# Windowed attention and a softplus feed-forward: every engine's order after slot 22 comes from a list scheduler in the kernel

## The chip, the cores and the metric

One core of one Trainium2 chip runs the whole program. The metric is the device time of one execution in microseconds (us). The kernel before took 929.23 us, the median of 3 runs (927.66 to 931.1).

## The reference, cut to what matters

```python
B, H, S, D = 8, 8, 576, 64           # float32; 4608 tokens in all
scores = q @ k.T / sqrt(D)           # per batch and head
# heads 0-3: the last 32 keys; heads 4-7: every 4th of the last 128 keys
attn = softmax(where(mask[h], scores, -1e9))
x = (attn @ v), heads side by side   # 4608 x 512
h = x @ w_in                         # 512 x 2048
g = maximum(h, 0) + log1p(exp(-abs(h)))
out = g @ w_out                      # 2048 x 512
```

## The kernel before, in words

The 4608 tokens are nine chunks of 512. A chunk has four attention groups (two heads each), 36 groups in all. A float32 matmul operand is split into a high and a low fp32r part, so a product is three matmuls: high by high, high by low, low by high. TensorE (PE) is the engine with the most work. W_in and W_out come in as 16 blocks (ff = 0 to 15) of 128 columns or rows.

**Chunks 0 to 2** run in 48 slots, (chunk, ff) pairs in the order of `RUNS`. A slot i is 12 matmuls of 512 columns for h (`h_part`, four times three) and 12 for the output of slot i - 2 (`o_part`, `LAG` = 2). Between them ScalarE (ACT) takes abs, exp and log of h, VectorE (DVE) makes softplus from them, ACT copies the high part gh, DVE subtracts to the low part gl. Chunks 0 and 1 leave their accumulators half way (`kept_part`, DRAM tile `kept`) and resume later (`resumed_part`). Slots 0 to 9 and all decoding of weights in that time follow the hand-written string `OPENING`.

**Chunks 3 to 8** run in three double passes (d = 0 to 2), two chunks at once. Each pass has eight pairs p; a pair has seven products (`product`, six matmuls each; seven instead of eight quarter products, by sums and differences of blocks of x and of W_in), whose results DVE takes out of two PSUM banks h_x and h_y into `temps`, `hs` or `stored` (`aside`). The output matmuls (`late_o`, 12 per use u of a W_out block) run beside them in the first half and alone in the second. The sums and differences of x (`combine`, `split_high`, `split_low`) must stand before the first pair of a pass; those of W_in (`weight_sum`, `weight_13`, `weight_24` on GpSimd, POOL, then copies on ACT and DVE) are made once per pair: pairs 0 to 3 during the slots (`EARLY` = 4), the rest during the first pass, then kept in DRAM and loaded for passes 1 and 2. W_out blocks are kept in DRAM by `keep_w_out` and streamed back into free buffers (`feed`, `used`).

**Attention** of groups 8 to 35 is done in visits. Visit n puts the scores of group n and the weighted values of group n - 1 into two halves of the same two PSUM banks `sv_ps`: 64 small matmuls of scores, then 64 of values. After it DVE scales and masks (`maximum`, L431) and takes maxima (L440), ACT takes eight exponentials (L448), DVE divides (L460, L463, L466) and transposes 32x32 blocks (L488); SP sends them to DRAM (`send`) and, when they have landed, brings them back rearranged (`bring`, four DMAs to tile pt). Visit n + 1 needs that pt for its values.

**What sets the order.** Every instruction of these engines stays in the order in which the kernel emits it, on its engine. The kernel before emits by clocks written by hand. `at(when, part)` puts a part on a heap by slot number, `pump` emits what is due, `tick` and `do_chores` add chores (decoding, sums, splits) while an estimated backlog of DVE is under 0.4 us. `attend` places the parts of a visit at fixed offsets; visits come every 3.3 slots (groups 8 to 11), 2.7 slots (groups 13 to 20), then every 20 us by `in_beats`. The output of a finished chunk leaves by `finished` (L1128): two column halves share one tile `ob` at a time ("w5_1", "x_d" for chunk 2), so the second pair of copies waits until the DMAs of the first have read it. All DMAs but two go through SP's queue, which waits for the semaphores of one DMA before it goes on to the next.

```python
at(clock(7.0 if quick else 5.5), g.divisor, cost=0.36)      # L959
at(clock(8.8 if quick else 8.2), send, n)                   # L965
at(clock(12.4 if quick else 13.0), bring, n)                # L966
```

Of the kernel before, what the change touches and what calls it, by code (L numbers as in the profile page):

```python
# [50 lines left out]
EARLY = 4  # L51
# [45 lines left out]
def tile_windowed_attention_softplus_ffn(  # L97
# [189 lines left out]
    def raw_block(d, name, kt):  # L287

        c = FIRST + 1 + 2 * d
        if name == "s1":  # L290
            if (d, kt) not in ones:
                if d == 0:
                    ones[d, kt] = const.tile([P, CH], F32, name="sums", tag=("g_x", "g_y")[kt])
                else:
                    if kt == 0:
                        ones[d] = const.tile([P, 2, CH], F32, name="sums", tag="w14_0")
# [31 lines left out]

    def blocks_of(d):

        def split(name):
            parts = []
            for kt in range(2):
                for cost, part in ((0.0, split_high), (0.69, split_low)):
                    chore = lambda part=part, kt=kt: part(d, name, kt)
                    chore.block = d, name
                    parts.append((cost, chore))
            return parts

        sums = lambda name: [(0.69, lambda kt=kt: combine(d, name, kt)) for kt in range(2)]  # L340
        before = split("a11") + split("a12")
        behind = sums("s1") + sums("s3") + sums("s2") + split("s2") + sums("s4")
        for name in ("s3", "s1", "a22", "s4"):
            behind += split(name)
        return before, behind
# [8 lines left out]
    class Group:  # L354
# [60 lines left out]
        def maximum(self):  # L415
# [24 lines left out]
            pin(nc.vector.tensor_reduce(out=nm, in_=self.blocks, axis=AX.X, op=ALU.max, negate=True))  # L440

        def exponentials(self):
            self.sm = wk.tile([P, NB], F32, name="sm")
            for t in range(NB):
# [76 lines left out]
        def weighted(self, shared=None):  # L521
# [24 lines left out]
            if self.c >= FIRST:  # L546
                self.x = x_half(self.c, self.pr // 2)[:, self.pr % 2], None, src
                return
# [14 lines left out]
        def x_high(self):  # L563
            for dh, _, src in self.x_parts():
# [107 lines left out]
    def ob_tiles(c, resumed=False):  # L672

        tags = ("x_c", "x_d")
        if resumed:
            tags = ("xh10", "xh11") if c else ("g_x", "g_y", "x_d")
        for m in range(NKT):
            if len(tags) == 3 and m < 2:
                obs[m] = const.tile([P, CH], F32, name="ob", tag=tags[m])
                continue  # L680
            if m % 2 == 0:
                obs["both"] = const.tile([P, 2, CH], F32, name="ob", tag=tags[-1] if m else tags[0])
            obs[m] = obs["both"][:, m % 2]
        for m in range(NKT if resumed else 0):
            load_dma(out=obs[m], in_=kept[c, m])

    def o_part(i, m):
# [5 lines left out]
        resumed = final and c < FIRST and ff == NFF - 1  # L693
        if first:
            o_ps[m] = bank(f"o_ps{m}", f"o{m}")
        if m == 0:
            if final and not resumed and c < FIRST:
                ob_tiles(c)
# [6 lines left out]
        if final and resumed:  # L705
            at(now[0] + 0.12, resumed_part, m, c, o_ps[m], cost=0.69)
        elif final and c == FIRST:
            at(now[0] + 0.25, finished, m, c, o_ps[m], cost=0.0 if m % 2 else 0.69)
        elif final and i + LAG <= OPENED:
            keeping[m] = c, o_ps[m]  # L710
        elif final:
            at(now[0] + 0.12, kept_part, m, c, o_ps[m])

    STEP = 2 / 7
# [66 lines left out]
    BEATS = 2 * NPAIR  # L781
# [6 lines left out]
    def weight_sum(p, j):  # L788
# [591 lines left out]
```

## Time and profile before

| what | value |
|---|---|
| median of 3 runs | 929.23 us (927.66 to 931.1) |
| the profiled execution | 932.48 us |
| its span, first to last instruction | 930.7 us |
| PE busy | 872.7 us, 94% of the span |
| DVE, ACT busy | 557.8 us (60%), 551.6 us (59%) |
| POOL busy | 56.0 us (6%) |
| moved by DMA | 177.54 MB, 191 GB/s over the span |
| mean granted TensorE clock | 0.967 |

The span is what the profiler sees between the first and the last instruction; the execution's own time is 1.8 us longer. A matmul's end is modelled, and matmuls overlap, so the busy time of PE holds more than its work: a matmul of 512 columns is shown with 0.39 us but starts 0.227 us after the one before it. The granted clock is 1 where TensorE ran at 2.4 GHz and 0.5 where it ran at 1.2 GHz; a mean between them says for what part of the stretch it was low.

### The profile page before, as it was taken

The numbers are of one execution on the slowest core, as the hardware profiler recorded it, in microseconds if no ns is written. First come the engines' busy times: TensorE is split into PE (matmuls) and PEld (weight loads), VectorE is DVE, ScalarE is ACT, GpSimd is POOL, SyncE is SP. The second block draws the span as 40 slices with busy tenths as digits, with TensorE's granted clock in tenths as the row PEclk, the third lists the DMA queues.
The fourth block names the chain that finished last, engine by engine and source line by source line (L and its number), as shares of the span: only waits on it lengthen the run. The fifth ranks groups of instructions, "written<-read, shape, count | busy, mean of one in ns | idle before, by whom it ended". The sixth has DMA issues, their size and how long they took to land.

```text
span 930.7 us, 19972 instructions
## 1 busy us (share of the span) xinstructions
PE 872.7 (94%) x7997; PEld 704.9 (76%) x7997; DVE 557.8 (60%) x950; ACT 551.6 (59%) x1354; POOL 56.0 (6%) x58
## 2 busy tenths in 40 slices
PE   6999999998998999899997799999998999999798
PEld 3788778886776887677875688778876888888686
DVE  5788978744544657766664555656655635555422
ACT  6888768764565666667565345666664435655421
POOL 0000000300004201431000000000000000000000
PEclk7899989999998999999999899999998999999999
DMA  7788725676657523766566646767743526562052
GB/s 245 252 258 266 244 68 190 193 259 226 205 173 257 202 82 117 264 225 225 171 205 231 211 147 190 265 227 250 259 151 128 182 80 205 190 204 69 23 203 91
DMA packets 91773, 177.54 MB, mean 191 GB/s; under 512 B 10144, under 2 KB 26656, under 8 KB 91680
## 3 DMA queue, kind: packets, MB, share of 16 engines
q1 hardware_dynamic: 91392, 175.86, 56.8%
q8 instruction: 63, 1.03, 0.4%
q10 hardware_dynamic: 288, 0.41, 0.1%
q14 instruction: 30, 0.25, 0.1%
HBM read 134.28 MB, written 41.94 MB: 189 GB/s over the span
## 4 chain that ended last, share of the span: by engine, by line
PE 71%; ACT 11%; DMA 8%; DVE 7%; issue 2%; SPq 1%; POOL 0%; DVEq 0%; ACTq 0%; POOLq 0%
PE o_ps L203 35%; PE h_ps L203 13%; PE h_x L203 9%; PE h_y L203 8%; PE sv_ps L203 5%; ACT s L448 3%; ACT e L1118 2%; DMA out_t<-ob 2%; DMA pt<-turned 2%; DMA raw<-w 2%; ACT e L1117 2%; ACT e L1119 2%; ACT gh L657 1%; DVE gl L663 1%; DVE hs L1113 1%
## 5 line engine op out<-in xcount | busy, mean ns | idle before, releaser
L203 PE MATMUL o_ps<-gh,t 128*128 128x512 f32 (+1 forms) x776 | 270.6, 396 | 19.5 <-DVE ob L1135 9.9
L203 PEld LDWEIGHTS o_ps<-gh,t 128*128 128x128 f32 x776 | 148.6, 192 | 53.3 <-ACT gh L657 11.7
L203 PE MATMUL o_ps<-gl,t 128*128 128x512 f32 (+1 forms) x388 | 153.5, 396 | 0.7 <-DVE gl L663 0.7
L203 PE MATMUL o_ps<-gh,parts 128*128 128x512 f32 x384 | 132.9, 402 | 0.0
L203 PE MATMUL h_ps<-xh,parts 128*128 128x512 f32 x384 | 132.6, 403 | 0.0
L203 PEld LDWEIGHTS o_ps<-gl,t 128*128 128x128 f32 x388 | 74.5, 192 | 17.7 <-DVE gl L663 2.5
L203 PEld LDWEIGHTS h_ps<-xh,parts 128*128 128x128 f32 x384 | 74.1, 193 | 16.0
L203 PEld LDWEIGHTS o_ps<-gh,parts 128*128 128x128 f32 x384 | 74.2, 193 | 16.0
L203 PE MATMUL o_ps<-gl,parts 128*128 128x512 f32 x192 | 76.5, 398 | 0.0
L203 PE MATMUL h_ps<-xl,parts 128*128 128x512 f32 x192 | 76.3, 397 | 0.0
L448 ACT ACTIVATE s<-s,nm 128x64 f32<-128x64 f32 x224 | 74.7, 336 | 1.4 <-DVE nm L440 0.4
L657 ACT CAST gh<-stored 128x512 fp32r<-128x512 f32 x48 | 29.8, 621 | 70.6 <-PE o_ps L203 70.5
L663 DVE TENSOR_TENSOR gl<-hs,gh 128x512 fp32r<-128x512 f32 x48 | 33.8, 704 | 62.1 <-ACT gh L657 61.6
L663 DVE TENSOR_TENSOR gl<-stored,gh 128x512 fp32r<-128x512 f32 x48 | 33.1, 690 | 59.9 <-ACT gh L657 59.8
L203 PE MATMUL h_x<-s,t 128*128 128x512 f32 x216 | 58.3, 407 | 11.2 <-DVE hs L1113 8.0
L1117 ACT ACTIVATE e<-hs 128x512 f32<-128x512 f32 x48 | 30.3, 631 | 64.9 <-DVE stored L1123 50.2
L1118 ACT ACTIVATE e<-e 128x512 f32<-128x512 f32 x96 | 60.7, 632 | 3.1
L1119 ACT ACTIVATE e<-e 128x512 f32<-128x512 f32 x96 | 60.7, 632 | 3.1
L203 PE MATMUL h_y<-s,t 128*128 128x512 f32 x216 | 56.1, 395 | 1.5 <-DVE temps L1113 0.7
L203 PEld LDWEIGHTS h_x<-s,t 128*128 128x128 f32 x216 | 40.5, 192 | 22.4 <-DVE hs L1113 10.1
L657 ACT CAST gh<-hs 128x512 fp32r<-128x512 f32 x48 | 29.3, 611 | 37.9 <-DVE hs L1123 37.9
L1117 ACT ACTIVATE e<-stored 128x512 f32<-128x512 f32 x48 | 30.2, 629 | 33.5 <-DVE stored L1113 32.5
(110 smaller groups left out, 1441.3 us busy)
## 6 DMA issues: line engine op xcount, KB each, us to landing
t<-w_out SPq DMA_DIRECT2D x132, 256.0 KB, 3.2
raw<-w SPq DMA_DIRECT2D x64, 256.0 KB, 4.6
v<-vp SPq DMA_DIRECT2D x28, 512.0 KB, 5.5
q<-qp SPq DMA_DIRECT2D x36, 256.0 KB, 3.8
turned_over<-w_one SPq DMA_DIRECT2D x18, 512.0 KB, 4.4
t<-w SPq DMA_DIRECT2D x18, 512.0 KB, 3.7
turned_over<-w_two SPq DMA_DIRECT2D x18, 512.0 KB, 4.4
w_out<-parts SPq DMA_DIRECT2D x16, 512.0 KB, 5.3
```

The lines of the kernel that those rows point to most:

```text
L203: return tc.keep_in_program_order(nc.tensor.matmul(**kw))
L448: pin(nc.scalar.activation(out=self.blocks[:, t], in_=src, func=AF.Exp, bias=self.nm[:, t : t + 1], scale=1.0 / 8.0 if self.masked else 1. ...
L657: pin((copy or nc.scalar.copy)(out=gh, in_=ready[i]))
L663: pin(nc.vector.tensor_tensor(out=gl, in0=e, in1=gh.bitcast(F32), op=ALU.subtract))
L1113: pin(nc.vector.tensor_tensor(out=dst, in0=banks[b], in1=temps[temp], op=ALU.add))
L1117: pin(nc.scalar.activation(out=e, in_=h, func=AF.Abs))
L1118: pin(nc.scalar.activation(out=e, in_=e, func=AF.Exp, scale=-1.0))
L1119: pin(nc.scalar.activation(out=e, in_=e, func=AF.Ln, bias=1.0))
```

## The change

The hand clocks now end at slot 22 (`HANDED`). Up to there the order is emitted as before, but visits 8 to 11 come every 2.95 slots instead of 3.3, and the writes of `keep_w_out` that began at slot 18 are gone from there. From slot 22 on, all remaining work is declared as tasks: engine, cost in us, the tasks it depends on, a rank, a ring of buffers that it takes. A loop then plays time forward. At each moment every free engine takes the open task of the lowest rank, and emits it, so each engine's order is that of the played times. PE chooses among three lists: the next visit if it is open and at least `VISIT_EVERY` = 14 us after the last; else the list of outputs (`second`) if it has fallen behind the count `upto` of the next h or product, else h and products (`first`); if the chosen list's head isn't open, the other. The played times use 0.227 us for a matmul, 0.62 to 0.71 us for an ACT or DVE instruction of 512 columns, and for a DMA 0.32 MB per us one after the other and 2.3 us to land. Writes that nobody waits for soon (rank 2 and over) start only while no DMA is under way in the played time.

Homes change too. The copies of a finished chunk go to two tiles ("w5_1" and "w3_1"), one for each pair of copies. `bring_kept` fetches the kept halves of chunk 0 to "g_x", "g_y" and the ring "a". The x tiles of chunks 3 to 8 take tags c, d, a, b instead of a, b, c, d. The sums of W_in for pairs from `EARLY` on use "x_a" and "x_b" instead of "x_c" and "x_d", and `EARLY` falls from 4 to 2. The number and shapes of the matmuls stay.

```diff
@@ -48,7 +48,9 @@
 HALF = CH // 2
 NPAIR = NFF // 2
 SQ = 32
-EARLY = 4
+EARLY = 2
+HANDED = 22
+VISIT_EVERY = 14.0
 NEG = -1.0e9
 DEPTH = 4
 THIN = 90
@@ -264,7 +266,7 @@
 
     def x_half(c, k):
         if (c, k) not in x_full:
-            tag = "x_" + "abcd"[2 * ((c - FIRST - 1) % 2) * (c > FIRST) + k]
+            tag = "x_" + ("abcd" if c == FIRST else "cdab")[2 * ((c - FIRST - 1) % 2) * (c > FIRST) + k]
             x_full[c, k] = const.tile([P, 2, CH], F32, name="x_full", tag=tag)
         return x_full[c, k]
...
+        if final and i < HANDED:
+            if i + LAG <= OPENED:
+                keeping[m] = c, o_ps[m]
+            else:
+                at(now[0] + 0.12, kept_part, m, c, o_ps[m])
...
-        last = i == len(slots) - 1
-        at(i + (0.9 if last else 1.0), softplus, i, cost=0.69)
-        if not last:
+        if i < HANDED - 1:
...
-                sums[p] = const.tile([P, 2, 2, HALF], F32, name="b", tag="x_c")
+                sums[p] = const.tile([P, 2, 2, HALF], F32, name="b", tag="x_a")
...
-        d = diffs[p] = dpool.tile(**shape, tag="a") if p < EARLY else const.tile(**shape, tag="x_d")
+        d = diffs[p] = dpool.tile(**shape, tag="a") if p < EARLY else const.tile(**shape, tag="x_b")
...
-    for ff in range(NFF):
-        at(18 + 0.8 * ff, keep_w_out, ff)
-    for p in range(NPAIR):
-        at(30 + 1.5 * p, keep_one, p)
-    double = (FIRST + 1) * NPR
-    attend(double, in_slots(23.4))
-    for j in range(1, 2 * NPR + 1):
-        attend(double + j, in_slots(26.2 + 2.7 * (j - 1)))
-    at(26.2, ob_tiles, 0, True)
...
+        attend(FIRST * NPR + j, 10.2 + 2.95 * j)
...
+    for i in range(OPENED + 1, HANDED):
...
+    pump(HANDED + 0.4)
+    assert not events and not chores
+
+    MM, LATENCY = 0.227, 0.06
...
+        def open(self, t):
+            return (
+                self.after <= t + 1e-9
+                and all(d.over(t) for d in self.deps)
+                and all(ring.open(t) for ring, _ in self.takes)
+                and (self.engine != SP or self.rank < 2.0 or arrived[0] <= t)
+            )
+
+    def run(task, t):
+        for ring, until in task.takes:
+            ring.take(until)
+        task.emit()
+        if task.engine == "SP":
+            free_at["SP"] = t + 0.08
+            arrived[0] = max(arrived[0], t) + task.cost / RATE
+            heapq.heappush(ends, arrived[0])
+            task.end = arrived[0] + LANDING
+        elif task.engine == "PE":
+            free_at["PE"] = t + task.cost
+            task.end = t + task.cost + 0.2 + LATENCY
+        else:
+            free_at[task.engine] = t + task.cost
+            task.end = t + task.cost + LATENCY
+        heapq.heappush(ends, task.end)
+        heapq.heappush(ends, free_at[task.engine])
+        if task.engine in queues:
+            queues[task.engine].remove(task)
+
+    RATE, LANDING = 0.32, 2.3
...
+    hs_ring, e_ring = Ring(3), Ring(2)
+    out_kept = [
+        Task(SP, 0.512, lambda ff=ff: keep_w_out(ff), rank=3.0 + 0.1 * ff, after=5.0 * ff + 2.0)
+        for ff in range(NFF)
+    ]
+    one_kept = [
+        Task(SP, 0.512, lambda p=p: keep_one(p), rank=5.0 + 0.1 * p, after=40.0 + 8.0 * p)
+        for p in range(NPAIR)
+    ]
...
+    def evacuation(c, m, done, tags, deps=()):
+
+        copied = Task(
+            ACT if m % 2 else DVE, 0.62 if m % 2 else 0.69, lambda: finished(m, c, tags),
+            [done, *deps], rank=-0.5,
+        )
+        evacuated[m] = copied
+        sent_out[c, m] = Task(SP, 0.256, lambda: send_out(m, c), [copied], rank=0.5)
...
+    def attention(n, since):
+
+        g = groups[n] if n < len(groups) else None
+        prev = visited.get(n - 1)
+        deps = [prev, brought.get(n - 1), scaled_of.get(n - 1), x_done.get(n - 2)]
+        if g:
+            deps += [loaded[n, "k"], loaded[n, "q"]]
+        deps += [loaded[n - 1, "v"]]
+        visited[n] = Task(None, 2.1 if g else 1.15, lambda: visit(n), deps, after=since)
+        visited[n].engine = "PE"
+        v = visited[n]
+        if n < len(groups):
+            loaded[n, "v"] = Task(SP, 0.512, groups[n].load_v, [v], rank=1.0)
+        if g:
+            scaled = Task(DVE, 0.69, g.maximum, [v, turned_of.get(n - 1), masks_in.get(g.c)], rank=0.25)
+            scaled_of[n] = scaled
+            great = Task(DVE, 0.69, g.greatest, [scaled], rank=0.26)
+        loads(n + 1)
+        prior = x_uses.get((n - 1) // 2, [])
+        x_done[n - 1] = Task(
+            ACT, 0.60, groups[n - 1].x_high, [v, scaled_of.get(n), *prior], rank=0.3
+        )
+        if not g:
+            return
+        exps = great
+        for t in range(NB):
+            exps = Task(
+                ACT, 0.34, lambda t=t: g.exponentials(slice(t, t + 1)), [great], rank=0.3 + 0.01 * t
+            )
+        last = Task(DVE, 0.40, g.divisor, [exps], rank=0.3)
+        over = Task(DVE, 0.70, lambda: g.divide(nc.vector), [last], rank=0.3)
+        turned = Task(DVE, 0.71, g.turn_squares, [over, sent_squares.get(n - 1)], rank=0.3)
+        turned_of[n] = turned
+        sent = Task(SP, 0.256, g.send_squares, [turned], rank=0.1)
+        sent_squares[n] = sent
+        brought[n] = Task(SP, 0.5, g.fetch_squares, [sent, v], rank=0.1)
...
+                n = 7 * p + k
+                spill = 2 * NKT if d == 0 else SPILL
+                base = given + 2 * NFF * NKT * d - spill
+                task.upto = base + (spill + NFF * NKT - REST) * n // (7 * NPAIR)
+                product_done[d, p, x] = product_done[d, p, weights] = task
...
+                asides[d, p, k] = Task(DVE, 0.70, emit, [task, before], rank=-1.0)
...
+                evacuation(uses[u][0], m, o, ("w5_1", "w3_1"), [
+                    *(sent_out[uses[u][0] - 1, m // 2 * 2 + k] for k in range(2)),
+                    *(product_done[0, q, n] for q in (NPAIR - 2, NPAIR - 1) for n in ("t1", "t3")),
+                ])
...
+        rank = 4.0 + 0.1 * p if p < 2 else 0.9
+        take = lambda over: [(hs_ring, over)] if p < EARLY else []
+        a = Task(POOL, 1.6, lambda: weight_sum(p, 0), deps, rank=rank, takes=take(one_over))
+        b = Task(POOL, 1.6, lambda: weight_sum(p, 1), [a], rank=rank, takes=take(two_over))
+        c = Task(POOL, 1.8, lambda: weight_13(p), [b], rank=rank, takes=take(d_over))
+        e = Task(POOL, 1.8, lambda: weight_24(p), [c], rank=rank)
...
+                for p in range(EARLY, NPAIR):
+                    prev = weights_of_pair(p, [prev, *(x_a_free + x_b_free)])
...
+    def choose(t):
+        if visits and t >= spaced and visits[0].open(t):
+            return visits
+        due = first and done_second < first[0].upto
+        for queue in (second, first) if due or not first else (first, second):
+            if queue and queue[0].open(t):
+                return queue
+
+    while first or second or visits or any(queues.values()):
+        t = clock[0]
+        for engine, queue in queues.items():
+            while free_at[engine] <= t + 1e-9:
+                task = min((k for k in queue if k.open(t)), key=lambda k: (k.rank, k.n), default=None)
+                if task is None:
                     break
-                now[0] = LATE + 2 * n + 0.25 * (m + 0.9)
-                spent = outputs(1)
-                behind += spent + pump(now[0] + 0.01) - 0.68
-                do_chores(now[0] + 0.01)
-    pump(LATE + 2 * DOUBLES * BEATS + 4)
-    while pending:
-        outputs(1)
-    pump(LATE + 2 * DOUBLES * BEATS + 8)
+                run(task, t)
+        if free_at["PE"] <= t + 1e-9 and (queue := choose(t)) is not None:
+            task = queue.pop(0)
+            run(task, t)
+            if queue is visits:
+                spaced = t + VISIT_EVERY
+            elif queue is second:
+                done_second += 1
+            continue
+        later = [k.after for q in queues.values() for k in q if k.after > t + 1e-9]
+        while ends and ends[0] <= t + 1e-9:
+            heapq.heappop(ends)
+        if not ends and not later:
+            raise RuntimeError("nothing can begin")
+        clock[0] = min(ends[:1] + later)
```

## Rows read from the trace of the kernel before

**Rows 1.** The page: busy time of the engines (share of the span, instructions), and PE's busy tenths and granted clock in 40 equal slices of the span.
```profile
PE 872.7 (94%) x7997; PEld 704.9 (76%) x7997; DVE 557.8 (60%) x950; ACT 551.6 (59%) x1354; POOL 56.0 (6%) x58
...
PE   6999999998998999899997799999998999999798
...
PEclk7899989999998999999999899999998999999999
```

**Rows 2.** The table of stretches by stage: stretch in us, its length, then busy time (instructions) of PE, PEld, DVE, ACT, POOL, granted clock, DMA share, GB/s. The stages are slots 10 to 21, slots 22 to 47, and the three double passes with the end.
```profile
93.60:172.50 78.90, 76.04 (x738) 62.24 (x736) 65.29 (x118) 59.92 (x149) 6.39 (x5) 0.96 0.53 173
172.50:348.90 176.40, 167.34 (x1777) 137.46 (x1776) 93.82 (x150) 103.78 (x281) 24.38 (x24) 0.96 0.58 198
348.90:556.10 207.20, 187.48 (x1740) 149.76 (x1739) 130.44 (x216) 122.30 (x302) 24.20 (x24) 0.97 0.60 202
556.10:749.70 193.60, 185.71 (x1681) 149.97 (x1680) 113.89 (x189) 110.88 (x266) 0.00 (x0) 0.97 0.60 199
749.70:930.70 181.00, 171.53 (x763) 141.13 (x762) 82.24 (x129) 83.13 (x136) 0.00 (x0) 1.00 0.41 137
```

**Rows 3.** The chain of work that ended last, in order of time: start us, us, what. Twelve output matmuls, a visit, and the twelve h matmuls behind it.
```profile
271.21 2.72 PE o_ps L203 x12
273.93 1.85 PE sv_ps L203 x117
275.78 2.97 PE h_ps L203 x12
```

**Rows 4.** Matmuls that write h_ps (12 to a slot, 48 slots) in the stretch from slot 22 on: stretch, length, PE busy (count), granted clock, DMA share, GB/s.
```profile
172.45:348.50 176.05, 78.36 (x312) 0.96 0.59 199
```

**Rows 5.** The last rows of the timeline.
```profile
926.26 0.28 PE L203 MATMUL o_ps<-gh,t 128*128 128x256 f32 x1
...
927.03 0.34 SPq L1261 DMA_DIRECT2D out_t<-pt  x1
```

**Rows 6.** What PE waited for from 172.5 us on: us in total, times, longest us.
```profile
PE o_ps L203 <- DVE ob L1135: 9.9, 2, 7.2
PE o_ps L203 <- ACT gh L657: 9.6, 5, 3.5
PE h_x L203 <- DVE hs L1113: 8.0, 5, 2.1
PE sv_ps L203 <- issue: 7.4, 2, 3.8
PE h_x L203 <- DVE temps L1113: 2.6, 1, 2.6
PE sv_ps L203 <- DMA pt<-turned: 1.6, 3, 1.0
```

**Rows 7.** The end of pass 0 in the chain of work that ended last: start us, us, what.
```profile
503.43 4.77 PE o_ps L203 x12
...
508.66 7.23 DMA out_t<-ob
...
516.01 0.70 DVE ob L1135
...
516.76 5.45 PE o_ps L203 x15
```

**Rows 8.** Instructions in order of time round the visits that start at 180.75 and 197.81 us: start us, us, engine, line, operation, [idle before it <- what ended that]. DVE from the scaling to the transposing, SP's send and fetch, and PE at the next visit.
```profile
182.74 0.69 DVE L431 SCALAR_TENSOR_TENSOR s<-sv_ps,mask 128x512 f32<-128x512 f32 x1 [1.49 <-PE sv_ps L203]
...
189.32 0.71 DVE L488 STREAM_TRANSPOSE squares<-s 128x512 f32<-128x512 f32 x1
...
190.06 0.32 SPq L138 DMA_DIRECT2D turned<-squares  x1
190.43 1.14 SPq L138 DMA_DIRECT2D w_out<-parts  x1
192.72 1.76 SPq L138 DMA_DIRECT2D pt<-turned  x4
...
198.60 1.14 PE L203 MATMUL sv_ps<-pt,v 64*64 64x32 f32 x64
```

**Rows 9.** The same round the visit that starts at 290.92 us: SP, then PE.
```profile
286.11 0.32 SPq L138 DMA_DIRECT2D turned<-squares  x1
...
289.62 3.04 SPq L138 DMA_DIRECT2D pt<-turned  x4
...
290.92 0.86 PE L203 MATMUL sv_ps<-k,q 64*32 64x64 f32 x64
295.43 2.32 PE L203 MATMUL sv_ps<-pt,v 64*64 64x32 f32 x64 [3.65 <-issue]
```

**Rows 10.** The chain round the visit that starts at 113.7 us (start us, us, what): the fetch of pt that ends its wait.
```profile
113.97 3.70 DMA pt<-turned
...
117.72 1.92 PE sv_ps L203 x60
```

**Rows 11.** POOL in order of time, the first and the last of its six instructions for the weights of pair 0.
```profile
278.54 2.89 POOL L797 TENSOR_TENSOR b<-parts 128x512 f32<-128x512 f32 x2 [95.89 <-DVE t L817]
...
283.84 1.07 POOL L811 TENSOR_TENSOR b<-b 128x256 f32<-128x256 f32 x1
```

**Rows 12.** POOL and DVE in order of time while the weights of a pair are made (start us, us, engine, line, operation).
```profile
287.46 2.89 POOL L797 TENSOR_TENSOR b<-parts 128x512 f32<-128x512 f32 x2 [2.56 <-DVE t L817]
...
289.10 1.80 DVE L663 TENSOR_TENSOR gl<-e,gh 128x512 fp32r<-128x512 f32 x1
```

More of the change, by code (lines that the diff above doesn't have):

```diff
@@ L327, in split_low @@
         ))
[L329 to L345, printed above, removed]
     def first_of(dil, t, g):
@@ L439, in maximum, with greatest, exponentials @@
                 beside.append(scaled)
[L440 to L444, printed above, removed]
+        def greatest(self):
+            pin(nc.vector.tensor_reduce(
+                out=self.nm, in_=self.blocks, axis=AX.X, op=ALU.max, negate=True
+            ))
+        def exponentials(self, part=slice(0, NB)):
+            if part.start == 0:
+                self.sm = wk.tile([P, NB], F32, name="sm")
+            for t in range(NB)[part]:
                 src = self.blocks[:, t]
@@ L1055, in do_chores @@
         behind = max(behind, 0.0)
-    def tick(time):
-        nonlocal behind
-        now[0] = time
-        behind += pump(time) - 0.69
-        do_chores(time)
-    for i in range(OPENED + 1, len(slots)):
+    for i in range(OPENED + 1, HANDED):
         for kt in range(NKT):
@@ new lines, in tile_windowed_attention_softplus_ffn @@
+    queues = {e: [] for e in ("DVE", "ACT", "POOL", "SP")}
+    free_at = dict.fromkeys(("PE", *queues), 0.0)
+    arrived = [0.0]
+    ends = []
+    def run(task, t):
[17 more added lines that the diff above has]
+            queues[task.engine].remove(task)
@@ new lines, in tile_windowed_attention_softplus_ffn, with chain_of_slot @@
+    first, second = [], []
+    h_done, low_done, o_done, plus_done = {}, {}, {}, {}
+    evacuated = {}
+    def chain_of_slot(i, begun):
+        plus = Task(DVE, 0.69, lambda: softplus(i), rank=0.5)
+        low = Task(DVE, 0.70, lambda: g_low(i), rank=0.8)
+        if begun is None:
+            plus.after = 1.9
+            e_ring.take(low)
+        else:
+            one = Task(ACT, 0.64, lambda: begin(i), [begun], rank=0.6, takes=[(e_ring, low)])
+            two = Task(ACT, 0.64, lambda: exp_of(i), [one], rank=0.5)
+            plus.deps.append(Task(ACT, 0.64, lambda: log_of(i), [two], rank=0.4))
+        high = Task(ACT, 0.63, lambda: g_high(i), [plus, o_done.get((i - 2, NKT - 1))], rank=0.7)
+        low.deps.append(high)
+        plus_done[i], low_done[i] = plus, low
@@ new lines, in tile_windowed_attention_softplus_ffn, with temps, product @@
+    product_done, asides = {}, {}
+    third_free, x_a_free, x_b_free = [], [], []
+    banks = {}
+    pair = {}
+    def temps(n):
+        if n < 2:
+            if "two" not in pair:
+                pair["two"] = const.tile([P, 2, CH], F32, name="temps", tag="xl01")
+            return pair["two"][:, n]
+        if "one" not in pair:
+            pair["one"] = const.tile([P, CH], F32, name="temps", tag="temps")
+        return pair["one"]
+    def product(d, p, name, x, b, begins):
+        if b not in banks:
+            banks[b] = bank(f"h_{'xy'[b]}", "h")
@@ L1182, in split_of @@
[L1182 to L1199 removed]
+    landed = {}
@@ new lines, in tile_windowed_attention_softplus_ffn, with __init__, over, giving @@
+    class Held:
+        def __init__(self, u):
+            self.ff, self.u = uses[u][1], u
+        def over(self, t):
+            return self.ff in held and landed[self.ff] <= t
+    def giving(what):
+        def emit():
+            for ff in what():
+                arrived[0] = max(arrived[0], clock[0]) + 0.512 / RATE
+                landed[ff] = arrived[0] + LANDING
+                heapq.heappush(ends, landed[ff])
+        return emit
+    SPILL, REST = 10, 12
+    given = NKT * (len(slots) - HANDED + LAG)
```

593 lines of the change are left out of this document (381 added, 212 removed).

## The prediction

> **What bounds the kernel now.** The page's first part comes first: PE is busy for 94% of the span, DVE and ACT for 60% and 59% [rows 1]. PE sets the time, and the question is what it loses. The 40 slices show where: PE falls to 9, 8 and 7 tenths in single slices, and the granted clock dips in or behind the same slices [rows 1]. A gap is paid twice, once as idle time and once at half speed after it.
>
> The table by stage turns that into a ledger [rows 2]. Against it I set the work that PE must do. Twelve matmuls of 512 columns take 2.72 us, so one takes 0.2267 us. A visit takes 1.85 us, and the twelve matmuls behind it 2.97 instead of 2.72 us, so a visit costs 2.10 us [rows 3]. Slot 22 starts at 172.5 us, and the 312 matmuls from there into h_ps are 26 slots of 12 [rows 4]. From there PE has 312 of h, 336 outputs of slots 20 to 47, 1008 of products (3 passes x 56 x 6) and 1152 outputs of the passes: 2808 x 0.2267 = 636.5 us. With 24 visits of 2.10 and a last one, values only, put at 1.3, it is 688.2 us. Without any loss PE would be done at 860.7 us; it is done at 926.5 (926.26 + 0.28, [rows 5]). The order costs 65.8 us at most. By stage:
>
> - slots 22 to 47: 624 matmuls and 9 visits, 160.3 of 176.4 us, 16.1 lost;
> - pass 0: 720 and 8 visits, 180.0 of 207.2, 27.2 lost;
> - pass 1: 720, 7 visits and the last, 179.2 of 193.6, 14.4 lost;
> - pass 2: 744 and none, 168.6 of 176.8, 8.2 lost.
>
> PE's waits from slot 22 on say what is late [rows 6]: outputs for the copy ob (9.9 us) and for gh (9.6), products for a bank that DVE has not emptied (hs 8.0, temps 2.6), visits for pt (7.4 shown as issue, and 1.6). That is 39 us of idle time. The rest is low clock and restarts. The chain at the end of pass 0 shows such a restart: 12 matmuls in 4.77 us after a wait, where 2.72 is usual, 2.05 us more; and behind it the largest single wait, a copy to ob that stands until the DMA of the copies before it has read the one tile, 7.23 us, then 15 matmuls in 5.45 us, 2.05 us more again [rows 7].
>
> **The change part by part.** The number and shapes of PE's matmuls stay, so the 688.2 us stay. What can change is the 65.8 us.
>
> *Two homes for the finished copies.* The wait of 7.23 us and its restart of 2.05 go, and so do the smaller waits for ob: 9.9 + 2.05 = 12 us. Next late there is gh, for which the same boundary waited just before.
>
> *The played order.* A list with a second list behind it lets PE do outputs where a product's bank isn't free, and products where gh isn't there. The waits for gh, hs and temps (20.2 us) and most restarts should go. I keep 5 us for places where both lists are closed (the start of each pass, where the sums of x must stand, and the hand-over of accumulators); the bounds are 0 and the 20.2 of today. I add 2.05 for one restart at low clock.
>
> *Visits.* PE is in order: a visit emitted before pt has landed stops everything behind it. The played chain from visit to visit is 2.1 + 0.26 for the visit, 0.75 twice for scale and maxima, 2.8 for exponentials, 0.46 + 0.76 + 0.77 for division and transposing, 3.1 for the send, 3.9 for the fetch: 15.6 us. Measured, the visit at 180.75 has its scaling at 182.74, its transposing done at 190.03, its send at 190.06, and the next visit's values start at 198.60 without a wait [rows 8]. From send to values that is 8.5 us at most, where the played times have 7.0. Beside other DMAs it is 9.3 (286.11 to 295.43, with 3.65 us of PE idle, [rows 9]). So a visit placed by the played times is between 0 and 2.4 us late. Today's waits for pt are 9.0 us in 25 visits, 0.36 each, at spacings of 17 us and more. I take 0.6 us, nearer to that row than to the late end, since writes that can wait stay behind in the played order: 25 x 0.6 = 15 us; the bounds are 0 and 60. What stands behind a late visit is all of PE; what hides nothing of it is the list, which is fixed by then.
>
> *Before slot 22.* Visit 9 moves up by 0.35 slots (3.30 to 2.95), 0.35 x 5.44 = 1.9 us, but the fetch it waits for lands at 117.7 us in either case [rows 10], so these 1.9 us are lost. Visits 10 to 12 then come 2.95 x 5.44 + 2.1 = 18.1 us apart, and the quiet chain needs 17.9 at most (180.75 to 198.60): nothing. The writes of W_out leave this stage, and SP with them; that costs nothing here, and after slot 22 they go where the played queue is empty.
>
> *Weights of pairs.* Pairs 2 and 3 move from the slots into pass 0. POOL's work for one pair takes 6.4 us (278.54 to 284.91, [rows 11]); ACT and DVE add some 3 us (estimate from three copies and three subtractions of 0.4 to 0.7 us). Six pairs one after the other at 9.4 us are ahead of products that use a pair in 7 x 1.36 + 8 x 0.68 + 2.1 = 17.1 us. Covered, with 7.7 us to spare per pair.
>
> While POOL makes sums, DVE slows: a subtraction of 512 columns is shown with 1.80 us beside POOL's sums [rows 12], where a DVE instruction of that size takes 0.69 in a quiet stretch [rows 8]. The Trainium skill (GPSIMD Engine Reference, section 1, Specifications) says that POOL shares its SBUF interfaces with VectorE and contends with DVE instructions of two SBUF inputs; that row agrees. By that rule two more pairs beside pass 0, whose DVE is the busiest of the later stages (130.44 of 207.20 us, [rows 2]), could cost up to 2 x 6.4 us halved, 6.4 us, if all of it delayed bank releases. The sum above leaves it out, because eight pairs run beside DVE before and after.
>
> **The sum**: residual 15 + 5 + 2.05 + 1.9 = 24 us of 65.8, a gain of 41.8. The profiled execution took 932.48 us by its own time, 1.8 over its span, and lies 3.25 us above the median. 932.48 - 41.8 = 890.7, less 3.25 is **887 us**, 4.5% faster.
>
> **The rivals.**
> *Late visits, still faster.* If 12 of 25 visits meet other DMAs as in [rows 9], that is 12 x 2.4 = 29 us, and three of them restart at low clock, 6; with the other 9 us the residual is 44 and the time 907 us. For it: the fetch alone takes 5.8 us there (289.62 to 295.43) where the played times have 3.9, and the writes of W_out, earlier spread from slot 18 on, all fall into the visits' time now. Against it: 20 of today's 25 visits from slot 22 on have no wait [rows 6]. The Trainium skill (DMA: Bandwidth & Descriptors, Latency and other measured facts) gives the HBM access as 0.2 us on average and 2 us at high load, which would make the constant 2.3 us for landing too short where it matters; the same rows agree in direction.
>
> *Only the homes help.* If data and not order make the other waits, only 12 us and a restart go: 929 - 14 = 915 us. Against it: products wait for DVE copies that stand behind other DVE work, which is order.
>
> *Slower: pair weights just in time.* With two pairs ahead instead of four, and one buffer pair x_a, x_b for the rest, every pair waits for the subtractions of the one before. If ACT and DVE, loaded by the passes, stretch a pair from 9.4 to over 17.1 us, products of pairs 2 to 7 wait six times. It decides from 25 us on: 6 x 7.9 = 47 us bring 887 to 934. For it: the doubled DVE time in [rows 12]. Against it: 15 us of added waiting per pair, on engines that are free a third of the time.
>
> *The change does nothing*, since the same chain of visits holds PE in either order: within 4.6 us of 929. Against it are the 30.1 us of waits that have nothing to do with visits.
>
> **How the numbers follow.** About 0.5% (4.6 us) is what a measurement of this kernel can tell from no change. Forecast 0.60; late visits 0.22; only the homes 0.07; these are faster, 0.88 after a little for the edge. No change 0.04. Slower 0.08. The range starts at 866, where only 2 us of the residual are left and nothing is late (932.48 - 65.8 + 2.6 - 3.25), and ends at 915 with the homes alone; outside it lie slower, no change, and a little at the lower edge.
>
> **What would show each step.** Right: no wait of PE for ob over 2 us; waits of PE for gh, hs and temps together under 8 us; waits at visits near 15 us in total, each under 2.5; slots 22 to 47 done in some 168 us, pass 0 in some 190; mean granted clock over 0.98. Late visits: waits for pt (or shown as issue in sv_ps) of 30 us or more, with low clock behind. Pair weights: PE waiting in products for t of L814 or L817 or for weights of pair 2 to 7. The forecast is wrong if PE's busy time, freed of low clock, is not what it was, or if idle time stays over 40 us.

## The result and the profile after

The changed kernel takes **865.12 us**, the median of 4 runs (862.41 to 868.45), where the kernel before takes 928.91 (4 runs, 927.66 to 931.1): ratio 0.9313, interval 0.9273 to 0.9352. The direction is as forecast. The forecast of 887 us is 22 us too slow, and the time lies 0.9 us under the low end of the range. The profiled execution took 866.28 us, the span 864.5.

The page's first part and its slices:

```profile
PE 848.7 (98%) x7997; PEld 692.5 (80%) x7997; DVE 565.0 (65%) x950; ACT 548.5 (63%) x1354; POOL 59.5 (7%) x58
...
PE   7899989999999999999999999999999999999998
...
PEclk7999989999999999999999999999999999999999
```

Against [rows 1]: from the seventh slice to the last but one PE has no 8 and no 7, and from the seventh on the clock has no dip. DVE and ACT are busy for about as long as before. PE has the same 7997 instructions and is busy for 24 us less: from slot 22 on 37.5 us of the span before stood at low clock, and none does now. The work did not become less; the gaps and the low clock behind them went.

The stretches after, cut at the same events as [rows 2] (start of slots 10 and 22, first product of each pass), with the same columns:

```profile
90.48:172.19 81.71, 78.56 (x865) 63.86 (x863) 68.09 (x124) 60.29 (x150) 5.62 (x4) 0.96 0.45 149
172.19:332.70 160.51, 160.51 (x1779) 131.97 (x1777) 92.86 (x150) 102.80 (x281) 19.31 (x18) 1.00 0.62 214
332.70:468.04 135.34, 135.34 (x1309) 111.17 (x1308) 109.39 (x179) 100.37 (x258) 33.56 (x30) 1.00 0.72 239
468.04:650.88 182.84, 182.21 (x1810) 149.62 (x1809) 123.01 (x201) 118.16 (x290) 0.00 (x0) 1.00 0.69 220
650.88:864.50 213.62, 209.75 (x937) 174.06 (x935) 99.78 (x151) 95.73 (x156) 0.00 (x0) 1.00 0.45 146
```

In the second and third stretch PE's busy time is the whole stretch, and the granted clock is 1.00 from slot 22 to the end. Slots 22 to 47 hold the same work as before (624 matmuls of 512 columns and 9 visits) and can be set against [rows 2] as they stand: 160.5 us instead of 176.4. The passes can't, since 180 output matmuls are put off from pass 0 to pass 2 and visits moved up: pass 0 is 72 us shorter and the last stretch 33 us longer. So their work is counted anew, with the forecast's prices:

- slots 22 to 47: 160.3 of 160.5 us, 0.2 lost, where 16.1 were lost before;
- pass 0: 540 matmuls and 6 visits, 135.0 of 135.3, 0.3 lost (27.2 before);
- pass 1: 720, 8 visits and the last, 181.3 of 182.8, 1.5 lost (14.4);
- pass 2: 924, 209.5 of 209.75, 0.3 lost (8.2).

PE's waits from slot 22 on, all there are (us in total, times, longest):

```profile
PE sv_ps L205 <- DMA pt<-turned: 0.5, 1, 0.5
PE o_ps L205 <- DVE gl L654: 0.2, 1, 0.2
```

The rows of [rows 6] add up to 39 us. The last rows answer to [rows 5]:

```profile
860.35 0.28 PE L205 MATMUL o_ps<-gh,t 128*128 128x256 f32 x1
...
861.12 0.34 SPq L1622 DMA_DIRECT2D out_t<-pt  x1
```

**The ledger.** From slot 22's first matmul (172.19 us) to the end of the last (860.63) are 688.4 us. One of the 24 visits now lies ahead of slot 22 (169.93 us), so the work left is 688.2 - 2.1 = 686.1 us. The order costs 2.3 us where it cost 65.8: 63.5 us come back. The stage ahead, with that visit more in it and 0.3 us shorter, gives 2.4, the tail behind the last matmul 0.3 (4.16 to 3.87): 66.2, which is 932.48 - 866.28. The 2.4 are less than what that stage scatters by (last section).

### The profile page after: what moved, and what is told of

The parts are those of the page before. It is cut to its first block, busy times and chain, and to the rows that moved or that the text cites. A ratio compares the mean times of both kernels' runs of the same rounds, so it can differ in the third digit from the quotient of the medians.

```text
span 864.5 us, 20007 instructions
## 1 busy us (share of the span) xinstructions
PE 848.7 (98%) x7997; PEld 692.5 (80%) x7997; DVE 565.0 (65%) x950; ACT 548.5 (63%) x1354; POOL 59.5 (7%) x58
## 3 DMA queue, kind: packets, MB, share of 16 engines
q1 hardware_dynamic: 90240, 172.19, 60.6%
## 4 chain that ended last, share of the span: by engine, by line
PE 89%; DMA 6%; ACT 2%; DVE 2%; issue 0%; SPq 0%; ACTq 0%
PE o_ps L205 44%; PE h_ps L205 14%; PE h_y L205 13%; PE h_x L205 13%; PE sv_ps L205 6%; DMA raw<-w 1%; DMA v<-vp 1%; DMA turned<-squares 1%; ACT s L437 1%; DMA pt<-turned 1%; DMA k<-kdl 1%; PE a_ps L205 0%; DMA mask<-cst 0%; DMA q<-qp 0%; DVE gl L654 0%
## 5 line engine op out<-in xcount | busy, mean ns | idle before, releaser
L205 PE MATMUL o_ps<-gh,t 128*128 128x512 f32 (+1 forms) x776 | 263.7, 389 | 0.0
L205 PEld LDWEIGHTS o_ps<-gh,t 128*128 128x128 f32 x776 | 145.2, 188 | 29.8
L205 PE MATMUL o_ps<-gl,t 128*128 128x512 f32 (+1 forms) x388 | 150.4, 388 | 0.2 <-DVE gl L654 0.2
L205 PE MATMUL o_ps<-gh,parts 128*128 128x512 f32 x384 | 130.3, 394 | 0.5 <-ACT ob L695 0.5
L205 PEld LDWEIGHTS h_ps<-xh,parts 128*128 128x128 f32 x384 | 72.6, 189 | 16.4 <-DVE e L636 0.9
L205 PE MATMUL h_x<-s,t 128*128 128x512 f32 x216 | 55.1, 390 | 0.0
L636 DVE SCALAR_TENSOR_TENSOR e<-h_ps,e 128x512 f32<-128x512 f32 x48 | 32.8, 685 | 27.3 <-ACT e L1091 23.4
L205 PEld LDWEIGHTS h_y<-s,t 128*128 128x128 f32 x216 | 40.3, 188 | 8.8 <-DVE hs L1342 0.4
```

The lines of the kernel that those rows point to most:

```text
L205: return tc.keep_in_program_order(nc.tensor.matmul(**kw))
L636: pin(nc.vector.scalar_tensor_tensor(out=e, in0=tiles.pop(i), scalar=0.0, in1=e, op0=ALU.max, op1=ALU.add))
```

## The experiments

"Stretch" below is the time in one profile from slot 22's first matmul to the start of the last: 753.8 us before, 688.2 after. The visit that moved ahead of slot 22 is 2.1 of the difference. Ratios are to the kernel before, measured again beside each run; where a kernel made from the changed one is told of, its time and stretch are set against 865.12 and 688.2. PE's waits are those from slot 22 on (41.9 us before, all kinds; 0.7 after).

How fine this tells things apart: the run of the section on visit 9, in which PE's order from slot 22 on is the same instruction for instruction, has a stretch of 687.2, 1.0 us off. For one home, the other list, the landing of 3.8 us and the ranks the interval of the ratio overlaps that of the change (0.9273 to 0.9352); that these four are slower rests on the stretch of one profile each.

### The homes of the finished copies

In the kernel before, two homes for the copies:

```diff
-tag="x_d" if c == FIRST else "w5_1"
+tag="x_d" if c == FIRST else ("w5_1", "w3_1")[m // 2]
```

> The kernel before, with one thing of the change: the copies of a finished chunk go to two tiles (w5_1 and w3_1) instead of one. Theory A (the played order brings the gain: PE always has an open task of one of its lists): only the waits for ob go, 9.9 us and one or two restarts of 2.05, so 913 to 918 us against 929, and the waits for gh, hs and temps (20 us) stay. Rival B (the new homes bring most of it): under 895 us, and the other waits shrink too.

The time is 916.0 us, ratio 0.9864 (0.9807 to 0.9920); stretch 742.7. The waits for ob are gone, the others stay nearly as in [rows 6]:

```profile
PE o_ps L203 <- ACT gh L657: 9.6, 5, 3.5
PE h_x L203 <- DVE hs L1113: 8.0, 5, 2.1
PE sv_ps L203 <- issue: 7.6, 2, 4.0
```

So the forecast's term of 12 us was right, and the one tile caused just that: the first expectation held. The reverse, the changed kernel with one home:

```diff
-("w5_1", "w3_1")
+("w5_1", "w5_1")
```

> The kernel after, with both pairs of finished copies in one tile (w5_1) as before; the played times do not know of it. Theory A: the wait for ob comes back at the ends of chunks, 7 us for the longest and 10 to 20 in all with restarts, so 875 to 885 us against 865. Rival B (homes bring most): 900 us or more. Rival C (nothing of the homes matters once outputs can give way): 865 to 868.

The time is 867.94 us, 0.9346 (0.9296 to 0.9396), within the third expectation; stretch 694.1. Of the 12 us that the tile cost in the hand-made order 3 are left by the time and 6 by the stretch. The order has not moved out of the way: PE, DVE and ACT do the same instructions in the same order as in the change from slot 22 on, since the played times do not know of the one tile. The copies do wait for the DMAs again, 16.8 us in nine of them, each 0.8 to 3.4 us (none in the change). But PE has other matmuls to do before it needs that bank, and only 1.5 us reach it, in two waits for ob; the wait in [rows 7] was 7.23 us, and outputs for that bank came next.

### The other list

PE may take only the list whose turn it is:

```diff
-for queue in (second, first) if due or not first else (first, second):
+for queue in (second,) if due or not first else (first,):
```

> The kernel after, where PE's choice does not turn to the other list when the head of the chosen one is not open: in the played times it waits. Theory A: PE's waits for gh, gl, hs and temps come back in part, 15 to 30 us, so 880 to 895 us. Rival D (fixed interleaving would do; the gain is in the order of DVE, ACT and the DMAs): within 3 us of 865.

The time is 871.23 us, 0.9383 (0.9339 to 0.9428); stretch 692.7, waits for gl 4.5 us in 3. Both expectations missed it, the one much too high, the other by 3 us. Stepping aside is worth 6 us by the time and 4.5 by the stretch, not the 20 that the waits for gh, hs and temps were before.

### How late a visit is placed

The played landing time of a DMA, 2.3 us, made shorter and longer:

```diff
-RATE, LANDING = 0.32, 2.3
+RATE, LANDING = 0.32, 0.8
```

> The kernel after, with the landing time of a DMA played as 0.8 us instead of 2.3. A visit needs two of them in a row (send, fetch), so it is emitted up to 3.0 us earlier relative to the data, where the trace of the kernel after shows pt landing 2.2 us ahead of its use on average. Theory A (the played DMA times give the slack): waits for pt at most visits, 1 us each on average, 20 to 30 us with restarts, so 885 to 895 us. Rival E (the slack comes from ACT, DVE and PE work around the visits, whatever DMA times are played): 865 to 870 us.

The time is 883.18 us, 0.9507 (0.9458 to 0.9556), 2 us under the first expectation's range; stretch 705.0. Now visits are late, as the forecast had feared for the change itself: by the landings in the trace pt comes after the values' start in 8 of 24, by up to 1.8 us. The row below counts single waits; its eight fall in six visits. Behind them 13.7 us run at low clock.

```profile
PE sv_ps L205 <- DMA pt<-turned: 6.3, 8, 1.6
PE o_ps L205 <- DMA t<-w: 1.9, 1, 1.9
PE o_ps L205 <- ACT gh L648: 1.1, 1, 1.1
```

With 3.8 in place of 2.3:

> The kernel after, with the landing time of a DMA played as 3.8 us instead of 2.3. Theory A: slack of the visits grows by up to 3 us, no wait for pt is left, and PE fills the time with the other lists; the last visit ahead of pass 0 comes some 20 us later (8 visits by 2.5 us), at about 333 us, so the first sums of x may be late by 5 to 10 us: 865 to 875 us. Rival F (visits bind nothing): 863 to 867.

The time is 870.54 us, 0.9376 (0.9324 to 0.9428), as expected; stretch 694.3. In the trace pt lands 4.5 us ahead of its use on average. The loss stands behind the start of pass 0, 3.7 us of waits for the splits of x (h_y for s of L322 and L326) and 6.8 us of low clock behind. Of the three values tried the change's 2.3 is the best.

The played queue of DMAs taken out, so that a DMA takes its own time whatever is ahead of it:

```diff
-task.end = arrived[0] + LANDING
+task.end = t + task.cost / RATE + LANDING
```

> The kernel after, where a played DMA no longer stands behind the ones issued before it: it ends its own transfer and 2.3 us after its issue. In the kernel after send to landing of pt takes 5.3 to 10.5 us, and 13 of 24 visits from slot 22 on need more than the 7.0 us that a lone pair of transfers is played with. Theory A (played DMA times, queue included, place each visit behind its data): these visits come 1 to 3 us too early, waits for pt 10 to 20 us with restarts, so 872 to 885 us. Rival E (other work around the visits gives the slack): 865 to 868.

The time is 872.2 us, 0.9402 (0.9359 to 0.9445), just inside the first expectation; stretch 696.2. But the waits for pt are 2.0 us and not 10 to 20: by the landings, 4 of 24 visits are late, by up to 0.8 us.

```profile
PE sv_ps L205 <- DMA pt<-turned: 2.0, 5, 0.6
PE h_y L205 <- ACT s L322: 1.7, 1, 1.7
PE h_y L205 <- DVE s L326: 1.2, 1, 1.2
```

The two waits for the splits of x (s) stand 4 us behind the start of pass 1. So the 7 us lie in part at the visits and in part there.

Writes that nobody waits for, let go at any time:

```diff
-and (self.engine != SP or self.rank < 2.0 or arrived[0] <= t)
+and True
```

> The kernel after, where writes that nobody waits for (W_out, W_in, sums) may start while other DMAs are under way in the played time. Theory A: the played times know of them too, so visits move later and PE does other work: within 5 us of 865. Rival C (keeping these writes out of the visits' way is what lets pt land in time): 875 us or more, waits for pt over 5 us.

The time is 874.92 us, 0.9429 (0.9386 to 0.9471); stretch 696.7. The size is what the second expectation gave, the place is not: pt 0.2 us, but 6.0 us of outputs waiting for gl, in two waits, one behind the start of pass 0 and one behind that of pass 1. Why the writes bring PE to gl too early stays open.

Visits at least 20 us apart instead of 14:

```diff
-VISIT_EVERY = 14.0
+VISIT_EVERY = 20.0
```

> The kernel after, with visits at least 20 us apart in the played times instead of 14. In the trace they come 16.4 to 23 us apart. Visit 20 then ends at 170 + 8 x 20 = 330 + 2 us instead of 315, and the sums of x behind it take some 9 us more, while the h of slot 47 ends at 328. Theory G: pass 0 starts late, 5 to 12 us of waits for the parts of s at h_y, 870 to 880 us. Rival F (visits bind nothing): 863 to 867 us.

The time is 872.63 us, 0.9415 (0.9363 to 0.9468); stretch 694.5, with 3.7 us of wait for the splits of x behind the start of pass 0, as the first expectation had it. Visits come 18.6 us apart on average in the change (16.4 to 23.5), 22.0 before: none comes as close as the constant of 14, so it does not decide. That the chain of a visit does is read from the code, not shown.

### Ranks, and the reserve of outputs

DVE, ACT, POOL and SP take the oldest open task, not the one of the lowest rank:

```diff
-key=lambda k: (k.rank, k.n)
+key=lambda k: k.n
```

> The kernel after, where every engine takes the oldest open task instead of the one of the lowest rank. Theory A (any order that is played with the right times keeps PE fed, since PE chooses among open tasks): 865 to 875 us. Rival D (priorities on DVE, ACT and SP are what keep banks and pt early): 885 us or more, with waits for hs, temps and pt.

The time is 870.48 us, 0.9392 (0.9337 to 0.9447), within the first expectation; stretch 693.0; one wait of 4.3 us for the splits of x, behind the start of pass 0. Ranks are worth some 5 us.

Outputs whenever one is open, instead of by the count `upto`:

```diff
-for queue in (second, first) if due or not first else (first, second):
+for queue in (second, first):
```

> The kernel after, where PE takes an output whenever one is open and h or a product only else; the count upto is not used. Theory G: PE is still fed from two lists with right times, but outputs are used up as soon as they open, so none is left to cover the start of a pass or a bank that is not empty: 868 to 880 us, with waits at h_x and h_y. Rival I (pacing by upto matters little): 863 to 867 us.

The time is 909.75 us, 0.9801 (0.9764 to 0.9837); stretch 723.3, from which 24 outputs (5.4 us) have moved ahead of slot 22. Both expectations fell: this alone gives back 45 us (the profiled execution, the quickest of four with 905.51 us, 39), with 27.7 us of waits, nearly all for what DVE and ACT have not made yet, and 24 us at low clock, which cost half of that. The largest waits:

```profile
PE o_ps L205 <- ACT gh L648: 6.8, 2, 4.1
PE h_ps L205 <- DVE e L636: 6.6, 3, 3.1
PE h_y L205 <- DVE e L636: 6.6, 1, 6.6
```

Its chain of work that ended last, where pass 0 begins (start us, us, what):

```profile
343.61 1.90 PE sv_ps L205 x117
...
347.36 2.66 ACT s L437 x16
...
352.41 1.93 DVE s L326 x2
...
355.00 2.93 PE h_y L205 x6
```

PE has used up the outputs that were ready, and the pass can't start before a visit's exponentials and the splits of x behind them are done. In the change the same place is, in order of time:

```profile
332.72 1.54 PE L205 MATMUL h_x<-a,parts 128*128 128x512 f32 x6
334.10 0.39 PE L205 MATMUL o_ps<-gh,parts 128*128 128x512 f32 x1
...
334.78 1.52 PE L205 MATMUL h_y<-s,t 128*128 128x512 f32 x6
```

Products and outputs that were kept back alternate. `upto` holds outputs back, and they are the cover here.

### The played costs

The costs of DVE, ACT and POOL in the played time, halved:

```diff
-free_at[task.engine] = t + task.cost
-task.end = t + task.cost + LATENCY
+free_at[task.engine] = t + 0.5 * task.cost
+task.end = t + 0.5 * task.cost + LATENCY
```

> The kernel after, where the played times give every DVE, ACT and POOL instruction half its cost; PE's and the DMAs' costs stay. Theory G (what brings the gain is that the played times are close to the chip's, for every engine): orders are made for engines twice as fast, so PE's next work is emitted before its inputs can stand; a visit's chain is played some 4 us short (half of 8.6 us from visit to send, less what is queueing), so waits at most visits, and waits for banks and gh: 895 to 930 us. Rival H (a list in the order of dependencies is enough, the costs hardly matter): 865 to 875 us.

The time is 985.64 us, ratio **1.0624** (1.0583 to 1.0665): slower than the hand-made order, and far above both expectations; stretch 805.2, with 82.8 us of waits, most of them products for banks that DVE has not emptied:

```profile
PE h_x L205 <- DVE temps L1342: 19.9, 9, 7.3
PE h_y L205 <- DVE temps L1342: 10.8, 9, 2.3
PE h_x L205 <- DVE temps L1344: 8.8, 9, 1.9
PE h_x L205 <- DVE hs L1344: 7.9, 9, 2.3
```

The loop is there, with both lists, ranks, homes and queue, and the gain is not. It hangs on the costs. How exact they must be, with 0.8 and 1.2 in the place of 0.5:

> The kernel after, where the played times give DVE, ACT and POOL instructions 0.8 of their cost. Theory G1 (the costs are near the chip's own durations and have no margin downwards): every bank and every gh is played 0.15 us per instruction too early; a fifth of the way to half costs is less than linear, as lists absorb some, so 875 to 900 us, with waits at h_x and h_y for temps and hs. Rival G2 (DMA and PE times set the order, these costs have slack): 865 to 870 us.

The time is 886.2 us, 0.9557 (0.9509 to 0.9605), as the first expectation had it; stretch 707.3, waits 11.8, the largest for banks (temps of L1342, 5.1 us in 3).

> The kernel after, where the played times give DVE, ACT and POOL instructions 1.2 of their cost. Theory G1 (one-sided: work played later than it is on the chip finds its inputs ready, and PE stands only where both lists are closed in the played times, which on the chip is no wait, since an order holds no times): 865 to 872 us, the start of pass 0 later by a few us. Rival G3 (any mismatch costs): 880 us or more.

The time is 883.07 us, 0.9515 (0.9466 to 0.9563); stretch 703.0, waits 10.4, the largest for gl, 5.8 us in 6. The first expectation, that long costs do little harm, fell: 18 us go, against 21 for costs that are too short. That the engines' orders are then out of step as well is the reading of those waits; it was not tested by itself.

### Visit 9

The one part ahead of slot 22: visits 8 to 11 at slots of their own, so that visit 9 doesn't come before its pt.

```diff
-attend(FIRST * NPR + j, 10.2 + 2.95 * j)
+attend(FIRST * NPR + j, (10.2, 13.9, 16.6, 19.2)[j])
```

> The kernel after, with the visits 8 to 11 placed by hand at slots 10.2, 13.9, 16.6 and 19.2 instead of 10.2, 13.15, 16.1 and 19.05. Visit 9 is the one visit at which PE still waits for pt (5.49 us for the visit instead of 1.85 in the profile of the kernel after, and 6.8 us at low clock behind it). Theory: 0.75 slots, 4.1 us of matmuls, go before it, and the low clock (up to 3.4 us) goes too: 3 to 6 us faster than the kernel after, 859 to 862 us. Rival: visit 10, now 2.7 slots behind, waits instead, and the time stays within 1 us of 865.

The time is 864.38 us, 0.9310 (0.9282 to 0.9338): the same as that of the change, as the rival said. All of PE's waits for pt from 80 us on, in the change (the first row) and here:

```profile
PE sv_ps L205 <- DMA pt<-turned: 3.0, 3, 1.4
```

```profile
PE sv_ps L205 <- DMA pt<-turned: 2.6, 1, 2.6
```

The wait moved, not to visit 10 as the rival had it, but to visit 11 (its values start at 147.66 us, the last part of pt lands at 150.44), with 6.8 us of low clock behind it. So this placing gains nothing.

## Why the prediction was too slow

**The ledger was right.** The 688.2 us of work and the bound of 65.8 us came true: 686.1 + 2.1 for the visit that moved, and 2.3 us lost. The time lies where the forecast put "nothing is late", which it took for the edge of the range. For the profiled execution it had 890.7 us, and 866.28 were measured. Of the 24.4 us between them 19.7 stand from slot 22 on (22.05 forecast, 2.3 lost), 4.3 ahead of it and 0.3 in the tail.

**The step that failed is the term for visits**, "a visit placed by the played times is between 0 and 2.4 us late", 25 x 0.6 = 15 us. Measured are 0.5 us of waits for pt in all. The lateness came from 8.5 us "from send to values" [rows 8], set against the 7.0 played. But 8.5 was only a bound, as the forecast itself says: the values were not waiting. By the landings in the same trace pt stood 5.9 us after that send, 2.6 us before the values, and for the 24 visits from there on send to last landing took 6.8 us on average (5.3 to 9.6), less than the 7.0. A visit of the change, SP and then PE (start us, us, operation):

```profile
230.71 0.32 SPq L140 DMA_DIRECT2D turned<-squares  x1
231.13 1.35 SPq L140 DMA_DIRECT2D ob<-kept  x3
234.01 1.75 SPq L140 DMA_DIRECT2D pt<-turned  x4
...
239.25 0.86 PE L205 MATMUL sv_ps<-k,q 64*32 64x64 f32 x64
240.04 1.14 PE L205 MATMUL sv_ps<-pt,v 64*64 64x32 f32 x64
```

From the send at 230.71 to the last landing of pt at 238.7 are 8.0 us, and the values start at 240.04, 1.4 us later. Worked out in this way for the 24 visits from slot 22 on (landings of the trace against the values' start), pt lands 0.8 to 4.3 us early in 22 and 0.17 and 0.64 us late in two; on average it is 2.2 us early. The chain did not get faster: send to landing takes 7.4 us on average (5.3 to 10.5) where it took 6.8 before. The forecast also set the played chain of a lone visit (7.0 us) against chains under load (up to 9.3). But the played time puts DMAs one behind the other too, at 0.32 MB per us, so under load the played visit moves back as well, and PE has other work meanwhile. The sign was wrong, not only the size. The runs show both parts. In the change the last of pt lands 2.3 us ahead of the values in the median of the 24 visits; without the played queue it is 1.4 us (4 late), with a played landing of 0.8 us it is 0.3 (8 late), with one of 3.8 us it is 4.25 (none late). So the landing constant matters more (18 us of time at 0.8) than the queue (7 us).

The Trainium skill (DMA: Bandwidth & Descriptors, Latency and other measured facts) has HBM access longer under load. In direction the trace agrees by its median alone: one fetch of pt takes 1.8, 2.6 and 6.0 us from issue to landing (least, median, most) where it took 1.8, 2.1 and 6.4 before, with pass 0 at a DMA share of 0.72 instead of 0.60. No run tells the HBM's part from that of other DMAs on the queue. That visits would be late by it did not follow.

**5 us for closed lists**: 0.2 measured. The starts of the passes show no wait. They are a weak place all the same: in the worsened kernels waits for the splits of x come up 4 to 14 us behind them (pass 0 with landing 3.8, no ranks, visits 20 us apart; pass 1 without the DMA queue).

**2.05 for a restart**: none; the granted clock is 1.00 from slot 22 on.

**1.9 us for visit 9** can't be settled: the stage ahead of slot 22 scatters by more (below). In this pair of profiles they were not lost. "Lands at 117.7 us in either case" was wrong: it landed at 112.9, 4.8 us earlier; 3.1 of them are there at the start of slot 10 already.

**The homes** were right as a term of the kernel before (12 us expected, 12.6 by the ratio), but not as a part of the whole: with the played order they are worth 3 to 6. None of these parts alone carries the gain: other list 6, DMA queue 7, held writes 10, ranks 5, homes 3 by the times. These don't add up to 65, and they need not: each takes one way of stepping aside from an order that has others. That is an argument; no run takes out two at once. Two things do carry it: costs that fit (halved, all of the gain and 57 us more are lost) and outputs held back as cover (45 us). The played costs do fit here: 0.227 us for a matmul against 0.2267 measured, and for DVE instructions of 512 columns 0.69 to 0.71 against these means (DVE from slot 22 on; count, then busy us and mean ns, then idle before):

```profile
L1364 DVE SCALAR_TENSOR_TENSOR hs<-hs,e 128x512 f32<-128x512 f32 x48 | 35.1, 731 | 2.9 <-ACT e L1360 2.9
...
L1344 DVE TENSOR_TENSOR temps<-h_x,temps 128x512 f32<-128x512 f32 x24 | 16.5, 689 | 12.3 <-PE h_x L205 11.8
```

**The rival of the pair weights** was not seen: no wait of PE for them. POOL has 18 instructions in slots 22 to 47 and 30 in pass 0, six to a pair, so of pairs 2 and 3 only pair 3 moved into pass 0. POOL in pass 0, the first instruction of four of the five pairs:

```profile
362.07 3.40 POOL L772 TENSOR_TENSOR b<-parts 128x512 f32<-128x512 f32 x2 [29.80 <-DVE t L792]
...
377.70 3.40 POOL L772 TENSOR_TENSOR b<-parts 128x512 f32<-128x512 f32 x2 [8.78 <-DVE parts L792]
...
387.56 2.51 POOL L772 TENSOR_TENSOR b<-parts 128x512 f32<-128x512 f32 x2 [2.50 <-DVE parts L792]
...
402.57 3.38 POOL L772 TENSOR_TENSOR b<-parts 128x512 f32<-128x512 f32 x2 [8.67 <-DVE parts L792]
```

A pair follows the one before after 9.9 to 15.6 us: more than the 9.4 estimated (POOL stands for DVE's subtractions before each), and less than the 17.1 that it may take. DVE is slowed beside POOL as [rows 12] showed, in single instructions of 1.1 to 1.8 us in this stretch; no bank was late for it, so the 6.4 us that the forecast set beside its sum cost nothing.

**The rivals "only the homes" and "late visits"** fall with the waits above. Not tried: which of the costs (DVE's, ACT's, POOL's) must fit best, and `EARLY` = 4 or the old homes of the x tiles and of the sums of W_in in the played order.

## What to carry to other kernels

Where one engine sets the time, count its work at the measured rate and take the difference from its time; a list scheduler that knows real durations won 63.5 of 65.8 us here, so put "nothing is late" inside the range and not at its edge. Where nobody waited, take a DMA's time from its landing, not from the start of the work that uses it. Before taking a term from the tail of a measured wait, ask whether the plan that is being judged would also move under that load. When such an order is made, measure the durations it plays (20% off, either way, cost 18 to 21 us of 865) and hold back ready work for the places where the rest of the work is short.

## What was not expected of the hardware

The same instructions up to slot 22 begin that slot between 168.0 and 174.8 us in twelve profiles of the changed kernel and its variants (all but "outputs whenever one is open" and "visit 9"). The place is the fetch of pt for visit 9: it lands between 110.9 and 115.6 us, 6.7 to 10.3 us after the send, and 0 to 6.8 us of low clock follow. So single runs differ by some 3 us to either side with no change in the code up to there, and a stretch between two matmuls of one profile tells small changes apart better than the time of a run.
